# Dense matmuls over all 128 rows beside windowed attention, with six PSUM banks for the attention and one mask per block

## The chip, the core and the metric

The kernel runs on one NeuronCore of a Trainium2 chip. The metric is the device time of one execution, in microseconds (us). Below, PE is the matrix engine, PEld its weight loads, DVE the vector engine, ACT the scalar engine, POOL the GpSimd engine, SP the engine whose queue issues most DMAs. PSUM has eight banks of 128 x 512 fp32, into which PE writes.

## What is computed

```
x = A_x                                        # 1 x 2048 x 512
g = sigmoid((x * gate_w).sum(-1))
a = x @ dft_hid_re.T ;  b = x @ dft_hid_im.T
A = dft_seq_re @ a - dft_seq_im @ b            # real part of a 2-D DFT
q, k, v = split(x @ wqkv)                      # 32 heads of 16
p = softmax(q k^T / 4, over keys 0..255 back)  # causal window of 256
B = (p v) @ wo
out = g * A + (1 - g) * B
```

## The kernel before

**Precision.** Every dense product is made from high and low parts: three matmuls per contraction chunk (`TERMS`), so a 128 x 512 result over 512 contractions takes twelve "terms" into one accumulator. `hi_of` makes the high part on ACT, `lo_of` the low part on DVE or POOL.

**Dense work** is a generator, `dense()`. It makes the q, k, v projections, then the hidden-dimension DFT (`b_group`, `a_group`), then 32 blocks of the sequence DFT (`c_block`, with `piece_load` and `piece_split` to bring and split the DFT matrix). One `next()` on the generator is one term. At the end `wo_run` multiplies by `wo`.

**Attention** runs in 128 block steps (8 groups of 4 heads times 16 blocks of 128 queries); `n` counts them. In step `n`, `s_head` makes the scores S of four heads for block `n` (a matmul of 48 rows in the upper or the lower 64 rows of PE), and a DVE instruction adds the window mask and takes the row extreme. Every fourth step `m_rows` turns the extremes of four blocks into rows: DVE, then a write to a small DRAM tile `m_scr`, then a read of it into two rows of `ring`. `LAG` = 9 steps later `t_head` makes the transposed scores T of the same block, whose matmul has 50 rows and adds the extreme by those two rows. ACT takes the exponential into `pt`, POOL zeroes what lies outside the window (`t_mask`), and every fourth step `pv` multiplies by v (96 small matmuls of 64 x 32, tile `o`).

**Beside attention** the dense terms are put between the S and T matmuls by `fill`: 16 terms in a step while `n < LAG`, 11.2 while the projections last, 5 during the sequence DFT. While the flag `rows[0]` is set, a term is two matmuls of 64 rows (upper and lower half of PE) into two PSUM banks; `collect` copies one bank by ACT and then DVE adds the other. Before and after attention a term is one matmul of 128 rows into one bank.

**PSUM.** Pool `ps_a` has four banks for S, T and the two sums of `pv`; pool `ps_d` has four for the dense accumulators.

**Order.** Instructions stand on each engine in the order in which the Python code issues them, and every engine works its list in order. `defer(t, f)` puts a function `t` ticks later; a dense term is one tick, a group of S and T adds 0.7, `pv` adds 9. `ld` issues a DMA on SP, and an SP entry whose condition isn't met holds up those behind it.

Of the kernel before, what the change touches and what calls it, by code (L numbers as in the profile page):

```python
# [15 lines left out]
P = 128  # L16
# [5 lines left out]
NH = 4  # L22
# [28 lines left out]
def fnet_window_mix(ctx: ExitStack, tc: tile.TileContext, xT, x, wqk, wv, wr, wi, cr, ci, wo, gw, out):  # L51
# [170 lines left out]
    rows = [False]  # L222
    turn = 0

    def acc():
        nonlocal turn
        if rows[0]:
            return [ps_d.tile([P, 512], F32, name=f"d{h}", tag=f"d{h}", bufs=2) for h in range(2)]
        turn ^= 1
        return [ps_d.tile([P, 512], F32, name="d0", tag=f"d{turn ^ 1}", bufs=2)]  # L230

    def mm(pss, w, x, start, stop):
        if len(pss) == 1:
            nc.tensor.matmul(pss[0], w, x, start=start, stop=stop)  # L234
        else:
            for h in range(2):
                r = slice(64 * h, 64 * h + 64)
                nc.tensor.matmul(pss[h], w[r], x[r], start=start, stop=stop)  # L238
        tick()

    def collect(pss, then, scale=1.0, tag="es"):
        t = pt_tile([P, 512]) if len(pss) == 1 else ev.tile([P, 512], F32, name=tag, bufs=3 if tag == "es" else 5)
        nc.scalar.activation(t, pss[0], AF.Copy, scale=scale)  # L243

        def add():
            nc.vector.scalar_tensor_tensor(t, pss[1], scale, t, op0=OP.mult, op1=OP.add)
            defer(3, then, t)
        if len(pss) == 1:
            defer(3, then, t)
        else:  # L250
            defer(3, add)

    def evict_split(pss, hi, lo, scale, done, pool=True):
# [7 lines left out]
        collect(pss, first, scale)  # L261

    def qk_evict(g, ss, i, pss):
# [6 lines left out]
        evict_split(pss, hl[:, 1 - i], hl[:, i], (-SCALE, 1.0)[i], done, i == 1)  # L270

# [11 lines left out]
    def qk_proj(g, ss, w):  # L283
        for i in range(2):
            pss = acc()
            n = 0
            for dk in range(DK):
                c = dk * 256 + i * 128
                for a, b in TERMS:
                    mm(pss, w[a][:, c:c + 128], XT[dk, ss][:, b], n == 0, n == 11)  # L290
                    n += 1
                    if n < 12:
                        yield
            qk_evict(g, ss, i, pss)
            yield
# [9 lines left out]

    def row_proj(sb, w, pss):
        n = 0
        ss, c = divmod(sb, 4)
        for dk in range(DK):
            wh = [w[dk // 2][h][:, (dk % 2) * 512:(dk % 2) * 512 + 512] for h in range(2)]  # L310
            for a, b in TERMS:
                mm(pss, XT[dk, ss][:, a, c * 128:(c + 1) * 128], wh[b], n == 0, n == 11)
                n += 1
                if n < 12:
                    yield

    def v_proj(sb, w):
        pss = acc()
        yield from row_proj(sb, w, pss)

        def done(t):
            (nc.sync if rows[0] else nc.scalar).dma_start(v_scr[sb // 4][sb % 4], t)
            have.add(("v", sb))
        collect(pss, done)
        yield
# [10 lines left out]
    def quarter_block(i, q, j, w, then):  # L336
        pss = acc()
        yield from row_proj(q + 4 * j, w, pss)
# [5 lines left out]
        collect(pss, kept, (1.0, -1.0)[i], "es" if j % 2 else "ev")  # L344
        yield
# [103 lines left out]
    def m_rows(u):  # L449
# [49 lines left out]

    def t_mask(n, p):  # L500
        w = min(WIN, S - n % NB * P)
        pt = PT[n]
        a = pt[:, 2 * p:2 * p + 2, 0:P]
        nc.gpsimd.affine_select(a, a, pattern=[[0, 2], [1, P]], compare_op=OP.is_ge, fill=0.0,  # L504
                                base=0, channel_multiplier=-1)
        if w == WIN:
            a = pt[:, 2 * p:2 * p + 2, 2 * P:3 * P]
            nc.gpsimd.affine_select(a, a, pattern=[[0, 2], [-1, P]], compare_op=OP.is_gt, fill=0.0,  # L508
                                    base=0, channel_multiplier=1)

    def pv(u, last=False):
# [17 lines left out]
        nc.scalar.copy(os, ot[0])  # L529
        defer(3, lambda: nc.vector.tensor_add(os, ot[1], os))  # L530
        hf = g // 4
# [26 lines left out]
        defer(7, o_out)  # L558

# [33 lines left out]
    def piece_split(n, at_=1, step=2):  # L593
# [8 lines left out]
        for k, j in enumerate((2, 1, 3)):  # L602
            d, src, sign = left(i, tb, raws, j)
            defer(at_ + step * k, minus if sign > 0 else plus, d, d, src, j != 3)
        defer(at_ + step * 3, lo_of, w[:, 0], main, hi, True)
        for k, d in enumerate((raws[0][:, HALVES[1]], raws[1])):
# [22 lines left out]
    def c_block(n, done, begin):  # L629
        i, tb = order[n]  # L630
        pss = acc()
        hl = PIECE.pop((i, tb))
        begin(tb)
        for m in range(12):
            q, t = divmod(m, 3)
            x, y = TERMS[t]
            mm(pss, hl[x][:, q * P:q * P + P], U[i, tb % 4, q][:, y], m == 0, m == 11)
            if m < 11:
                yield
        if FIN:  # L640
            wo_run()
        done(tb, pss)
        piece_split(n + 2, 2, 2)
# [5 lines left out]
    def dense():  # L649
# [82 lines left out]

        def store_r(tb, pss):
            t = ev.tile([P, 512], F32, name="ev")
            nc.scalar.activation(t, pss[0], AF.Copy, scale=g1[:, tb:tb + 1])

            def add():
                nc.vector.scalar_tensor_tensor(t, pss[1], g1[:, tb:tb + 1], t, op0=OP.mult, op1=OP.add)
            if len(pss) == 2:
                defer(3, add)  # L740
            defer(7, ld, r_scr[0][tb], t)

# [5 lines left out]

        def add_r(tb, pss):
            r = R.pop(tb)  # L750
            for ps in pss:
                nc.vector.scalar_tensor_tensor(r, ps, g1[:, tb:tb + 1], r, op0=OP.mult, op1=OP.add)
            if FIN and tb in (11, 15):
# [90 lines left out]
    def wo_run():  # L844
# [11 lines left out]
        for q in range(0, 512, w):  # L856
# [3 lines left out]
            for g in range(NG):  # L860
                for a, b in TERMS:
                    mm([ps[:, :w]], OHL[sb][g][:, a, c * P:(c + 1) * P], WO[g][b][:, k], n == 0, n == 11)
                    n += 1
# [47 lines left out]
    for n in range(N + LAG + 1):  # L911
        k = n - LAG
        ring_ahead(n + 1)
        if k in (-2, 0):
            v_ahead(k // 2 + 1)
        for p in range(NH):
            if 0 <= k < N > n:
                s_head(n, p)
                t_head(k, p ^ 1)
            elif p % 2 == 0:  # L920
                for j in range(p, p + 2):
                    if n < N:
                        s_head(n, j)
                    elif k < N:
                        t_head(k, j)
# [6 lines left out]
            if p == 2 and k % 4 == 0:  # L932
                if k >= 4:
# [14 lines left out]
    with tc.If(small < 1):  # L948
        OTHER.clear()
        QT = {}  # L950
        for i in range(2):
# [6 lines left out]
            for tb in range(16):  # L958
                raws = raw_tiles(i, tb)
                dh, dl = (pt_tile([P, 3, 512], F32R) for _ in range(2))  # L960
                for j in (1, 2, 3):
# [3 lines left out]
                    lo_of(dl[:, j - 1], d, dh[:, j - 1])  # L965
                pss = acc()
                for n in range(36):
                    q, j = n % 4, n // 4 % 3
                    x, y = TERMS[n // 12]
                    mm(pss, (dh, dl)[x][:, j, q * P:q * P + P], QT[i, j, q][:, y], n == 0, n == 35)  # L970
# [3 lines left out]
                nc.vector.scalar_tensor_tensor(r, pss[0], g1[:, tb:tb + 1], r, op0=OP.mult, op1=OP.add)  # L974
                ld(o, r)
# [45 lines left out]
```

## Time and profile before

| | |
|---|---|
| median of 3 runs | 777.09 us (772.69 to 777.9) |
| the profiled execution: its own time | 772.52 us |
| the profiled execution: span from first to last instruction | 770.8 us |
| PE busy | 650.1 us, 84% of the span |
| DVE / ACT / POOL busy | 544.1 / 437.8 / 470.4 us |
| mean granted PE clock | 0.906 |
| DMA | 174.36 MB, mean 226 GB/s |

The time outside the span is 1.7 us. Busy times overlap, and the busy time of PE includes the modelled tail of each matmul, so that it overstates what PE does. The span has four stages, by what runs beside attention: start-up to 34.6 us; attention's first nine steps, S alone, to 71.4; attention beside projections and the hidden DFT to 353.8; attention beside the sequence DFT to 677; then the rest without attention.

### The profile page before, as it was taken

What the parts mean: (1) busy time and instruction counts of PE and PEld (TensorE: products, weight loads), DVE (VectorE), ACT (ScalarE), POOL (GpSimd) and SP (SyncE); (2) the same over time, 40 slices, a digit from 0 to 9 for tenths busy, and PEclk for the clock granted to TensorE, in tenths of its full rate; (3) what the DMA queues carried; (4) which work ended last, traced back from release to release, by engine and by line L of the source; (5) the groups of instructions that cost most, each with busy time, mean ns of one, the idle gap of its engine ahead of it and who ended that gap; (6) DMA issues with size and microseconds to landing.
All of it is one profiled execution on the core that took longest, in us unless ns stands there. A gap on an engine that the chain in (4) does not pass through costs nothing.

```text
span 770.8 us, 18841 instructions
## 1 busy us (share of the span) xinstructions
PE 650.1 (84%) x6558; PEld 499.8 (65%) x6558; DVE 544.1 (71%) x1471; ACT 437.8 (57%) x928; POOL 470.4 (61%) x718
## 2 busy tenths in 40 slices
PE   9999999899999999978677978878887687835976
PEld 6788887777788777766455655655555456624754
DVE  5388878898897889768567757676678863516554
ACT  6334775455576545666577657656756567514230
POOL 5002565667667878787768859796875869822000
PEclk9999999999999999989789879978978868975979
DMA  7857775777666877798868678885877648697675
GB/s 281 264 171 221 221 233 174 214 215 219 212 206 194 236 211 216 251 277 251 254 182 248 220 203 248 263 247 148 269 205 242 209 162 301 233 297 259 189 249 155
DMA packets 99994, 174.36 MB, mean 226 GB/s; under 512 B 34420, under 2 KB 35316, under 8 KB 99764
## 3 DMA queue, kind: packets, MB, share of 16 engines
q1 hardware_dynamic: 98452, 170.98, 72.2%
q10 hardware_dynamic: 1440, 2.10, 0.8%
q8 instruction: 54, 0.88, 0.5%
q14 instruction: 48, 0.39, 0.2%
HBM read 114.03 MB, written 63.46 MB: 230 GB/s over the span
## 4 chain that ended last, share of the span: by engine, by line
DMA 18%; PE 17%; POOL 8%; DVE 8%; issue 6%; SPq 4%; ACT 3%; DVEq 0%; POOLq 0%; ACTq 0%
DMA ring<-m_scr 5%; PE d L238 5%; SPq L97 4%; PE t L234 4%; DVE sm L445 3%; PE o L523 3%; DMA raw<-cr 3%; DMA ring<-qk_scr 3%; PE t L497 2%; DMA pt<-o_scr 2%; PE s L442 2%; POOL pt L504 1%; POOL hl L106 1%; DMA hl<-cr 1%; DMA ev<-wo 1%
## 5 line engine op out<-in xcount | busy, mean ns | idle before, releaser
L445 DVE CUSTOM_DVE_ANT_0 sm<-s,mask 128x384 f32<-128x384 f32 (+2 forms) x512 | 269.8, 527 | 87.0 <-PE s L442 41.9
L498 ACT ACTIVATE pt<-t 128x384 f32<-128x384 f32 (+2 forms) x512 | 234.2, 475 | 131.8 <-PE t L497 93.7
L497 PE MATMUL t<-ring,ring 50*128 50x384 f32 (+2 forms) x512 | 199.9, 400 | 56.6 <-DMA ring<-m_scr 32.0
L442 PE MATMUL s<-ring,ring 48*128 48x384 f32 (+2 forms) x512 | 185.0, 372 | 24.2 <-DVE nm L445 22.5
L504 POOL TENSOR_SCALAR_AFFINE_SELECT pt<-pt 128x256 f32<-128x256 f32 x256 | 116.0, 454 | 124.2 <-ACT pt L498 117.0
L238 PE MATMUL d<-big,hl 64*128 64x512 f32 x896 | 171.8, 421 | 0.0
L497 PEld LDWEIGHTS t<-ring,ring 50*128 50x128 f32 x512 | 101.9, 202 | 89.0 <-issue 26.5
L442 PEld LDWEIGHTS s<-ring,ring 48*128 48x128 f32 x512 | 99.4, 198 | 78.7 <-DVE nm L445 66.3
L238 PE MATMUL d<-hl,big 64*128 64x512 f32 x984 | 147.9, 395 | 0.0
L238 PE MATMUL d<-big,es 64*128 64x512 f32 x448 | 122.7, 473 | 0.0
L238 PEld LDWEIGHTS d<-big,hl 64*128 64x128 f32 x896 | 110.0, 198 | 5.2 <-issue 0.6
L238 PEld LDWEIGHTS d<-hl,big 64*128 64x128 f32 x984 | 105.2, 186 | 6.9 <-issue 0.8
L508 POOL TENSOR_SCALAR_AFFINE_SELECT pt<-pt 128x256 f32<-128x256 f32 x224 | 95.3, 425 | 0.0
L523 PE MATMUL o<-pt,vpad 64*32 64x320 f32 (+5 forms) x2816 | 83.3, 373 | 5.9 <-DVE nm L445 3.7
L523 PEld LDWEIGHTS o<-pt,vpad 64*32 64x32 f32 x2816 | 66.6, 113 | 28.1 <-DVE nm L445 10.3
L238 PEld LDWEIGHTS d<-big,es 64*128 64x128 f32 x448 | 66.3, 224 | 2.5 <-issue 0.6
L106 POOL TENSOR_TENSOR hl<-es,hl 128x512 fp32r<-128x512 f32 x14 | 19.0, 1359 | 65.2 <-ACT hl L103 61.6
L529 ACT COPY os<-o 128x512 f32<-128x512 f32 x32 | 18.8, 587 | 64.2 <-PE o L523 64.2
L530 DVE TENSOR_TENSOR os<-o,os 128x512 f32<-128x512 f32 x32 | 22.1, 690 | 42.8 <-ACT os L529 38.8
L106 POOL TENSOR_TENSOR hl<-raw,es 128x512 fp32r<-128x512 f32 x32 | 44.0, 1375 | 0.0
L243 ACT ACTIVATE es<-d 128x512 f32<-128x512 f32 x53 | 31.7, 598 | 19.8 <-PE d L238 19.0
L106 POOL TENSOR_TENSOR big<-big 128x512 fp32r<-128x512 f32 x32 | 41.6, 1304 | 0.2 <-ACT big L103 0.2
(100 smaller groups left out, 902.5 us busy)
## 6 DMA issues: line engine op xcount, KB each, us to landing
qk_scr<-hl SPq DMA_DIRECT2D x32, 512.0 KB
ring<-qk_scr SPq DMA_DIRECT2D x128, 128.0 KB
ring<-qk_scr SPq DMA_DIRECT2D x128, 64.0 KB
u_scr<-os SPq DMA_DIRECT2D x32, 256.0 KB
raw<-cr SPq DMA_DIRECT2D x16, 512.0 KB
big<-cr SPq DMA_DIRECT2D x16, 512.0 KB
raw<-ci SPq DMA_DIRECT2D x16, 512.0 KB
big<-ci SPq DMA_DIRECT2D x16, 512.0 KB
```

The source lines that it names most:

```text
L97: nc.sync.dma_start(dst, src)
L106: (nc.gpsimd if pool else nc.vector).tensor_sub(lo, raw, f(hi))
L234: nc.tensor.matmul(pss[0], w, x, start=start, stop=stop)
L238: nc.tensor.matmul(pss[h], w[r], x[r], start=start, stop=stop)
L243: nc.scalar.activation(t, pss[0], AF.Copy, scale=scale)
L442: nc.tensor.matmul(ps[:, :w], ring[0][r, p, jb * P:(jb + 1) * P], ring[1][r, p, k0:k0 + w], start=True, stop=True)
L445: nc.vector.tensor_tensor_reduce(out=sm[:, :w], in0=ps[:, :w], in1=mask[:, WIN - w:], scale=1.0, scalar=3e38, op0=OP.add, op1=OP.min, accu ...
L497: nc.tensor.matmul(ps[:, :w], ring[1][r, p, q0:q0 + P], ring[0][r, p, q0:q0 + w], start=True, stop=True)
L498: nc.scalar.activation(pt[:, j, :w], ps[:, :w], AF.Exp, scale=-1.0)
L504: nc.gpsimd.affine_select(a, a, pattern=[[0, 2], [1, P]], compare_op=OP.is_ge, fill=0.0, base=0, channel_multiplier=-1)
L508: nc.gpsimd.affine_select(a, a, pattern=[[0, 2], [-1, P]], compare_op=OP.is_gt, fill=0.0, base=0, channel_multiplier=1)
L523: nc.tensor.matmul(ot[h][32 * j:32 * j + 32, a - sb * 512:e - sb * 512], v2[r, j], pt[r, j, a - kb * P:e - kb * P], start=kb == kbs[0], st ...
```

## The change

1. A dense term is one matmul of 128 rows into one bank all the time; the DVE addition of the second half is gone (`mm`, `collect`, `store_r`, `add_r`). The pool `ps_d` has two banks.
2. `ps_a` has six banks.
3. A step has two groups and not four: each issues S, T, S, T for two heads and then the dense terms of half a step (`fill` adds `2 * rate` once per group).
4. `t_mask` masks four heads at once: two POOL instructions of 4 x 128 per row and step where four of 2 x 128 were.
5. The reads of `m_scr` into `ring` are issued on ACT and not on SP.
6. Some delays move: the addition of the two `pv` sums from 3 to 5 ticks, its store from 7 to 9; in `piece_split` the low part is taken before the sums and differences.

```diff
-    ps_a = ctx.enter_context(tc.tile_pool(name="ps_a", bufs=4, space=PSUM))
+    ps_a = ctx.enter_context(tc.tile_pool(name="ps_a", bufs=6, space=PSUM))
...
     def acc():
-        nonlocal turn
-        if rows[0]:
-            return [ps_d.tile([P, 512], F32, name=f"d{h}", tag=f"d{h}", bufs=2) for h in range(2)]
-        turn ^= 1
-        return [ps_d.tile([P, 512], F32, name="d0", tag=f"d{turn ^ 1}", bufs=2)]
-
-    def mm(pss, w, x, start, stop):
-        if len(pss) == 1:
-            nc.tensor.matmul(pss[0], w, x, start=start, stop=stop)
-        else:
-            for h in range(2):
-                r = slice(64 * h, 64 * h + 64)
-                nc.tensor.matmul(pss[h], w[r], x[r], start=start, stop=stop)
+        return ps_d.tile([P, 512], F32, name="d")
+
+    def mm(ps, w, x, start, stop):
+        nc.tensor.matmul(ps, w, x, start=start, stop=stop)
         tick()
...
-        nc.scalar.activation(t, pss[0], AF.Copy, scale=scale)
-
-        def add():
-            nc.vector.scalar_tensor_tensor(t, pss[1], scale, t, op0=OP.mult, op1=OP.add)
-            defer(3, then, t)
...
+        nc.scalar.activation(t, ps, AF.Copy, scale=scale)
+        defer(3, then, t)
...
                 for h in range(2):
-                    ld(f(ring[0][64 * h + 48:64 * h + 50, :, b % NB * P:b % NB * P + (e - b) * P]),
-                       ms[:, h, :, o:o + e - b].rearrange("l p b i q -> l p (b i q)"))
+                    nc.scalar.dma_start(f(ring[0][64 * h + 48:64 * h + 50, :, b % NB * P:b % NB * P + (e - b) * P]),
+                                        ms[:, h, :, o:o + e - b].rearrange("l p b i q -> l p (b i q)"))
...
-    def t_mask(n, p):
+    def t_mask(n):
...
-        a = pt[:, 2 * p:2 * p + 2, 0:P]
-        nc.gpsimd.affine_select(a, a, pattern=[[0, 2], [1, P]], compare_op=OP.is_ge, fill=0.0,
+        a = pt[:, :, 0:P]
+        nc.gpsimd.affine_select(a, a, pattern=[[0, 4], [1, P]], compare_op=OP.is_ge, fill=0.0,
                                 base=0, channel_multiplier=-1)
...
         def add_r(tb, ps):
             r = R.pop(tb)
-            for ps in pss:
-                nc.vector.scalar_tensor_tensor(r, ps, g1[:, tb:tb + 1], r, op0=OP.mult, op1=OP.add)
+            nc.vector.scalar_tensor_tensor(r, ps, g1[:, tb:tb + 1], r, op0=OP.mult, op1=OP.add)
...
-        quota += rate / 2
+        quota += 2 * rate
...
-        for p in range(NH):
-            if 0 <= k < N > n:
-                s_head(n, p)
-                t_head(k, p ^ 1)
...
-            if p % 2 and 0 <= k < N:
-                defer(2, t_mask, k, p // 2)
-            tick(0.7)
-            fill(n)
...
+        for p in (0, 2):
+            for j in (p, p + 1):
+                if n < N:
+                    s_head(n, j)
+                if 0 <= k < N:
+                    t_head(k, j ^ 1)
+            tick(1.4)
+            if p and 0 <= k < N:
+                defer(4, t_mask, k)
```

On PE in the stage of the projections, before: `s` and `t` are S and T, and two neighbouring numbers of `d` are the two banks of one dense accumulator, so each term is a row with the lower number and one with the higher.

```order
L442 MATMUL s<-ring_281,ring_280 128x384
L497 MATMUL t<-ring_280,ring_281 128x384
L238 MATMUL d_5172<-hl,big 128x512
L238 MATMUL d_5173<-hl,big 128x512
L238 MATMUL d_5172<-hl,big 128x512
L238 MATMUL d_5173<-hl,big 128x512
L238 MATMUL d_5241<-hl,big 128x512
L238 MATMUL d_5242<-hl,big 128x512
L442 MATMUL s<-ring_281,ring_280 128x384
```

The same engine and stage with the change; a row with x6 is six terms, each of 128 rows.

```order
L227 MATMUL d<-big,hl 128x512 x6
L424 MATMUL s<-ring_281,ring_280 128x384
L479 MATMUL t<-ring_280,ring_281 128x384
L424 MATMUL s<-ring_281,ring_280 128x384
L479 MATMUL t<-ring_280,ring_281 128x384
L227 MATMUL d<-big,hl 128x512 x5
```

Where PE had matmuls in one half of its rows throughout, it now goes from 128-row terms to four half-row matmuls and back, twice in a step.

On SP in the stage of the sequence DFT, before: from the write of one `m_scr` tile to its read.

```order
L97 DMA m_scr_179<-mt 4x32x32
L97 DMA u_scr_1_203<-os 128x512
L97 DMA vr<-v_scr_110 128x4x64
L97 DMA r_scr_3_213<-ev 128x512
L97 DMA raw<-cr 128x1024
L97 DMA big<-cr 128x1024
L97 DMA hl<-ci 128x512
L97 DMA ring_280<-m_scr_179 2x2x512 x2
L97 DMA ring_280<-qk_scr_3_3_93 32x2x512
```

The read of the same tile with the change stands on ACT, among the exponentials (`pt<-t`) and the casts:

```order
L103 CAST es<-raw 128x512
L480 ACTIVATE pt<-t 128x384 x2
L103 CAST big<-big 128x512
L480 ACTIVATE pt<-t 128x256 x2
L450 DMA ring_280<-m_scr_179 2x2x512 x2
L480 ACTIVATE pt<-t 128x256 x2
L103 CAST big<-big 128x512
```

The read has left SP's list, where it stood behind three loads of the DFT matrix (512, 512 and 256 KB by the profile's list of DMAs), and now stands between exponentials on ACT.

More of the change, by code (lines that the diff above doesn't have):

```diff
@@ L222, in fnet_window_mix, with collect, evict_split @@
     rows = [False]
-    turn = 0
     def acc():
-        nonlocal turn
-        if rows[0]:
-            return [ps_d.tile([P, 512], F32, name=f"d{h}", tag=f"d{h}", bufs=2) for h in range(2)]
-        turn ^= 1
-        return [ps_d.tile([P, 512], F32, name="d0", tag=f"d{turn ^ 1}", bufs=2)]
-    def mm(pss, w, x, start, stop):
-        if len(pss) == 1:
-            nc.tensor.matmul(pss[0], w, x, start=start, stop=stop)
-        else:
-            for h in range(2):
-                r = slice(64 * h, 64 * h + 64)
-                nc.tensor.matmul(pss[h], w[r], x[r], start=start, stop=stop)
-        tick()
-    def collect(pss, then, scale=1.0, tag="es"):
-        t = pt_tile([P, 512]) if len(pss) == 1 else ev.tile([P, 512], F32, name=tag, bufs=3 if tag == "es" else 5)
-        nc.scalar.activation(t, pss[0], AF.Copy, scale=scale)
-        def add():
-            nc.vector.scalar_tensor_tensor(t, pss[1], scale, t, op0=OP.mult, op1=OP.add)
-            defer(3, then, t)
[L248 to L253, printed above, removed]
+        return ps_d.tile([P, 512], F32, name="d")
+    def mm(ps, w, x, start, stop):
+        nc.tensor.matmul(ps, w, x, start=start, stop=stop)
+        tick()
+    def collect(ps, then, scale=1.0, tag="es"):
+        t = ev.tile([P, 512], F32, name=tag, bufs=3 if tag == "es" else 5) if rows[0] else pt_tile([P, 512])
+        nc.scalar.activation(t, ps, AF.Copy, scale=scale)
+        defer(3, then, t)
+    def evict_split(ps, hi, lo, scale, done, pool=True):
         def first(t):
@@ L260, in second, with qk_evict @@
             defer(6, done)
-        collect(pss, first, scale)
-    def qk_evict(g, ss, i, pss):
+        collect(ps, first, scale)
+    def qk_evict(g, ss, i, ps):
         hl = ev.tile([P, 2, 512], F32R, name="hl", bufs=3)
@@ L284, in qk_proj @@
         for i in range(2):
-            pss = acc()
+            ps = acc()
             n = 0
@@ L293, in qk_proj @@
                         yield
-            qk_evict(g, ss, i, pss)
+            qk_evict(g, ss, i, ps)
             yield
@@ L317, in v_proj @@
     def v_proj(sb, w):
-        pss = acc()
-        yield from row_proj(sb, w, pss)
+        ps = acc()
+        yield from row_proj(sb, w, ps)
         def done(t):
@@ L323, in done @@
             have.add(("v", sb))
-        collect(pss, done)
+        collect(ps, done)
         yield
@@ L336, in quarter_block @@
     def quarter_block(i, q, j, w, then):
-        pss = acc()
-        yield from row_proj(q + 4 * j, w, pss)
+        ps = acc()
+        yield from row_proj(q + 4 * j, w, ps)
         def kept(t):
@@ L343, in kept @@
             then(t)
[L344 removed]
+        collect(ps, kept, (1.0, -1.0)[i], "es" if j % 2 else "ev")
         yield
@@ L603, in piece_split @@
             d, src, sign = left(i, tb, raws, j)
-            defer(at_ + step * k, minus if sign > 0 else plus, d, d, src, j != 3)
-        defer(at_ + step * 3, lo_of, w[:, 0], main, hi, True)
+            defer(at_ + step * (k + 2), minus if sign > 0 else plus, d, d, src, j != 3)
+        defer(at_ + step, lo_of, w[:, 0], main, hi, True)
         for k, d in enumerate((raws[0][:, HALVES[1]], raws[1])):
@@ L630, in c_block @@
         i, tb = order[n]
-        pss = acc()
+        ps = acc()
         hl = PIECE.pop((i, tb))
@@ L641, in c_block @@
             wo_run()
-        done(tb, pss)
+        done(tb, ps)
         piece_split(n + 2, 2, 2)
@@ L731, in begin_0, with store_r @@
             pass
-        def store_r(tb, pss):
+        def store_r(tb, ps):
             t = ev.tile([P, 512], F32, name="ev")
[L735 to L741, printed above, removed]
+            nc.scalar.activation(t, ps, AF.Copy, scale=g1[:, tb:tb + 1])
+            defer(5, ld, r_scr[0][tb], t)
         R = {}
@@ L915, in fnet_window_mix @@
             v_ahead(k // 2 + 1)
-        for p in range(NH):
-            if 0 <= k < N > n:
-                s_head(n, p)
-                t_head(k, p ^ 1)
[L920 to L925, printed above, removed]
-            if p % 2 and 0 <= k < N:
-                defer(2, t_mask, k, p // 2)
-            tick(0.7)
-            fill(n)
+        for p in (0, 2):
[7 more added lines that the diff above has]
+                defer(4, t_mask, k)
             if p == 0 and k % 4 == 0 and k // 4 - 1 in ML:
                 defer(3, m_rows, k // 4 - 1)
-            if p == 2 and k % 4 == 0:
+            if p and k % 4 == 0:
                 if k >= 4:
@@ L973, in fnet_window_mix @@
                 ld(r, o)
-                nc.vector.scalar_tensor_tensor(r, pss[0], g1[:, tb:tb + 1], r, op0=OP.mult, op1=OP.add)
+                nc.vector.scalar_tensor_tensor(r, ps, g1[:, tb:tb + 1], r, op0=OP.mult, op1=OP.add)
                 ld(o, r)
```

26 lines of the change are left out of this document (13 added, 13 removed).

## The prediction

> **What bounds the kernel now.** I read the busy times by stage first, and in the same windows the S matmuls, the dense terms and the sums of v (columns: window, its length, busy us and count, granted clock, DMA share, GB/s).
>
> ```profile
> core 0: us, PE busy (x) PEld busy (x) DVE busy (x) ACT busy (x) POOL busy (x), PEclk, DMA share, GB/s
> 34.60:71.38 36.78, 36.78 (x315) 30.64 (x316) 29.78 (x97) 12.69 (x23) 2.93 (x3) 1.00 0.66 215
> 71.38:353.80 282.42, 261.74 (x3201) 219.99 (x3198) 236.31 (x692) 176.00 (x374) 199.18 (x321) 0.99 0.72 217
> 353.80:677.00 323.20, 255.82 (x2692) 177.99 (x2688) 218.75 (x598) 207.19 (x474) 248.75 (x377) 0.85 0.76 230
> ...
> 71.38:353.80 282.42, 84.60 (x248) 0.99 0.72 217
> 353.80:677.00 323.20, 93.16 (x228) 0.85 0.76 230
> ...
> 71.38:353.80 282.42, 218.40 (x1392) 0.99 0.72 217
> 353.80:677.00 323.20, 169.38 (x672) 0.85 0.76 230
> ...
> 71.38:353.80 282.42, 34.66 (x1312) 0.99 0.72 217
> 353.80:677.00 323.20, 48.62 (x1504) 0.85 0.76 230
> ```
>
> The first window (S alone) is all PE. In the second (projections) PE and DVE are both above 80% busy, at full clock. In the third (sequence DFT) nobody is above 79%, and the clock is 0.85. Four S make a step: 62 steps in the second window, 57 in the third, plus nine of T alone. What PE really works is found from starts, not from busy time. The timeline of PE has the three forms side by side:
>
> ```profile
> 34.66 0.33 PE L442 MATMUL s<-ring,ring 48*128 48x128 f32 x2
> 34.92 2.10 PE L234 MATMUL d<-hl,big 128*128 128x512 f32 x8
> 36.96 0.33 PE L442 MATMUL s<-ring,ring 48*128 48x128 f32 x2
> ...
> 41.34 0.28 PE L442 MATMUL s<-ring,ring 48*128 48x256 f32 x2
> 41.46 2.03 PE L238 MATMUL d<-big,hl 64*128 64x512 f32 x16
> ...
> 47.34 0.34 PE L442 MATMUL s<-ring,ring 48*128 48x384 f32 x2
> 47.52 1.99 PE L238 MATMUL d<-hl,big 64*128 64x512 f32 x16
> 49.34 0.34 PE L442 MATMUL s<-ring,ring 48*128 48x384 f32 x2
> ...
> 121.72 2.42 PE L523 MATMUL o<-pt,vpad 64*32 64x64 f32 x96
> 124.07 0.50 PE L238 MATMUL d<-hl,big 64*128 64x512 f32 x2
> ```
>
> From 47.34 on, everything is in half rows: two S of 384 columns start 0.18 us ahead of the dense terms, and eight terms (x16) take 1.82 us, **0.228 each**. At 41.34 two S of 256 columns take 0.12, so two of 128 take 0.06. The first group is just what the change makes everywhere: two S of 128 columns, then eight terms of 128 rows. It takes 36.96 - 34.66 = 2.30 us; in half rows it would be 0.06 + 1.82 = 1.88. **Leaving the 128-row form and coming back costs 0.42 us a group**, some 0.21 a switch. The terms themselves cost the same: two half-row matmuls of a pair run at once.
>
> So PE works, in the second window, 696 terms x 0.228 + 248 pairs of S and T x 0.18 + 14 pv (1312 / 96) x 2.5 (121.72 to 124.07, and the switch behind it) = 159 + 45 + 35 = 239 of 282 us, and idles 43. In the third, 336 x 0.228 + 264 x 0.18 + 16 x 2.5 = 164 at full clock, 193 at 0.85, of 323. What PE waits for, in the second window and then in the third, and the chain of the third:
>
> ```profile
> PEld s L442 <- DVE nm L445: 21.5, 38, 1.4
> PEld t L497 <- DVE nm L445: 7.6, 9, 2.2
> ...
> PE t L497 <- DMA ring<-m_scr: 27.6, 11, 7.0
> PEld s L442 <- DVE nm L445: 44.8, 94, 4.1
> POOL pt L504 <- ACT pt L498: 58.3, 41, 4.6
> ...
> by line: DMA ring<-m_scr 12.8%; issue 10.8%; SPq L97 8.9%; PE d L238 7.6%; PE o L523 7.2%; DVE sm L445 5.4%; PE t L497 4.8%; DMA ring<-qk_scr 3.5%; PE s L442 3.1%; POOL pt L504 2.9%; ACT pt L498 2.3%; POOL pt L508 2.2%; DVE ev L752 2.2%; PO
> ```
>
> In the projections PE waits mostly for a bank that DVE has not read. In the sequence DFT the dearest link is the read of `m_scr`, in front of T; PE's own work is 22.7% of the chain, 73 us.
>
> **The switches (added).** A step has two groups, each out of the 128-row form and back. A step with `pv` goes term, S and T, `pv`, term: three switches there, where before it had two.
> - First window: 9 steps x 2 x 0.42 = 7.6. PE is busy without a gap, so all of it counts: **+7**. The ends are 0 and +8.
> - Second: 62 x 4 - 14 = 234 switches x 0.21 = 49 us. PE would work 239 + 49 = 288 us in a window of 282, so it can't be hidden whole. PE becomes the only bound, and the 43 us of idling shrink: the waits for banks (29 us in the two rows above) are what the six banks and a lighter DVE take away. I leave 12 us of idling: 300, **+18**. The ends are +6 (no idling) and +49 (all idling stays).
> - Third: 132 groups x 2 - 16 = 248 x 0.21 = 52, at clock 0.85 61 us. Of PE's 193 us here 73 are on the chain, 38%; the same share of the switches is **+23**. The ends are 0 (hidden in PE's 130 us of idling) and +61.
>
> The Trainium skill ("TensorEngine Tiling", Key Properties) says that a change of tiling mode drains the array, a change of tile within it does not; that speaks against this change. Its "TensorE: Matmul & The Clock Gate" puts a load of 128 columns at 107 ns (LDWEIGHTS) and the drain at some 175 ns (Single matmul latency); from these one switch is an estimated 0.28 us, by which the second window's 49 us would be 66. Here the trace agrees that the array drains, but has 0.42 us for two, and that is used.
>
> **Taken from DVE.** The second halves' additions go:
>
> ```profile
> L246 DVE SCALAR_TENSOR_TENSOR es<-d,es 128x512 f32<-128x512 f32 x53 | 36.3, 685 | 3.3 <-ACT es L243 3.0 <-PE d L238 0.3
> L738 DVE SCALAR_TENSOR_TENSOR ev<-d,g,ev 128x512 f32<-128x512 f32 x16 | 11.9, 745 | 0.0
> L752 DVE SCALAR_TENSOR_TENSOR ev<-d,g,ev 128x512 f32<-128x512 f32 x28 | 20.8, 742 | 23.3 <-PE d L238 8.8 <-DMA ev<-r_scr 6.8 <-DMA lt<-l_scr 5.0
> ```
>
> In the projections that is 53 x 0.685 and 16 more of the same: 47 us of DVE's 236, which lies beside PE's 288 and so shortens nothing by itself; it is counted in the shrunk idling. In the third window all of L738 and twelve of L752's 28 go, 21 us of 219, and with the latter part of their 2.2% of the chain (7 us): **-4**; the ends are 0 and -7.
>
> **Six banks.** In the third window S waits 44.8 us for DVE, but only 5.4% of the chain (17 us) is DVE's reduction. More banks move the wait and don't make DVE faster: **-5**; the ends are 0 and -17.
>
> **The read of `m_scr` on ACT.** Two pieces of the chain of the third window, the slow case and the fast one, and what SP waited for:
>
> ```profile
> 394.26 5.55 DMA ring<-m_scr
> ...
> 473.27 1.59 DMA ring<-m_scr
> ...
> SPq L97 <- DMA m_scr<-mt: 18.6, 14, 3.2
> ...
> q1 hardware_dynamic: 98452, 170.98, 72.2%
> q10 hardware_dynamic: 1440, 2.10, 0.8%
> ...
> L322 ACTq DMA_DIRECT2D v_scr<-pt x6: 326/326/361, 15.7 to 34.7; - x6
> ```
>
> The same 8 KB take 5.55 us from issue to landing behind other loads and 1.59 alone. ACT's DMAs are in a queue of their own (q10), nearly empty. If the read lands in 1.6 us, eleven waits of 27.6 us in all shrink by up to 3-4 us each: **-22**, leaving the tail of the 7.0. The ends are 0 (it waits in the same 16 engines) and -41, its whole 12.8%. What is added: 80 issues of some 0.33 us in ACT's list, 26 us where ACT is 64% busy, beside PE; and ACT now stands still until the write has landed, with exponentials behind it, whose banks PE's T needs. The read is 12 ticks behind the write, in the third window more than a step (323 / 66 = 4.9 us), so I cost it at nothing; if ACT arrives as early as SP did, it is the 18.6 us of SP's row.
>
> The Trainium skill ("DMA: Bandwidth & Descriptors", Issuing engines are not separate DMA queues) says that all issuers' DMAs run on the same 16 engines and that another issuer saves issue time only. By that the -22 would be nearly 0, and the whole sum some 22 higher; the two rows of the chain show a spread to win, but no read from ACT beside heavy loads.
>
> **One mask for four heads.** These are the sizes that the trace has:
>
> ```profile
> L504 POOL TENSOR_SCALAR_AFFINE_SELECT pt<-pt 128x256 f32<-128x256 f32 x256 | 116.0, 454 | 124.2 <-ACT pt L498 117.0 <-DMA ring<-qk_scr 7.0
> L186 POOL TENSOR_SCALAR_AFFINE_SELECT mask<-mask 128x384 f32<-128x384 f32 x1 | 0.6, 646 | 0.1
> L188 POOL TENSOR_SCALAR_AFFINE_SELECT mask<-mask 128x384 f32<-128x384 f32 x1 | 0.8, 845 | 0.1
> ```
>
> From 0.454 us for 256 columns and 0.646 or 0.845 for 384, 512 columns are bounded by 0.65 (no further growth) and 1.24 (the steeper slope on). Against two of 0.454 that is -0.26 to +0.33 for each of 240 masks, -62 to +79 us of POOL. I take no change, the middle: the gentler slope gives 0.84. What POOL may gain is its standing before masks whose exponentials aren't there (58.3 us in the third window), since the one mask comes later. It is 77% busy there, and its masks are 5.1% of the chain, 16 us; 0.65 or 1.24 in place of 0.91 would make that -5 or +6, and the value is 0.
>
> **Moved delays and two accumulators instead of four** in the last stage: a block of twelve terms takes 2.7 us, an eviction 0.74. Nothing.
>
> **Sum**, against the profiled execution: 772.5 + 7 + 18 + 23 - 4 - 5 - 22 = 789.5. The runs' median, 777.09, is 4.6 above that execution, which is as fast as the fastest run; I add half of it: **792 us**.
>
> **Rivals.**
> - *The sequence DFT gains more than PE loses.* PE idles 130 of 323 us there, so the switches may hide whole, while the reads and banks give all they cost: -27.6 and -17 and -4, about -49, held by POOL's 249 busy us. With +7 and +6 ahead of it: 772.5 - 36 + 2 = 739. It decides from the point at which the third window falls by more than the first two grow (25 us): then the kernel is faster. For it: the clock is 0.85 because PE stands still there, and each removed wait also keeps the clock up. Against it: PE's matmuls stand in one list, and a switch delays the S that DVE waits for. Chance 0.20; its milder part, 745 to 767.
> - *A switch is cheaper behind wider matmuls.* The price comes from S of 128 columns; S and T are mostly 384 wide, and if the weights load while they run, only one switch in two costs: +4, +0 (263 us of PE work in 282), +11 - 31 in the third, 758. Against it: the switch from S to terms shows a load at its full price after the drain. Chance 0.06.
> - *ACT stands still.* The read waits on ACT as on SP, 18.6 us, and lands no sooner: no -22, so 792 + 41 = 833. Chance 0.10.
> - *The terms cancel*: the second window at its lower end (+6) and the third at -14: within 1%. Chance 0.14.
> - The forecast, slower by 8 to 50 us: 0.50.
>
> **How the numbers follow.** One per cent (7.8 us) is about what a measurement of this kernel can tell from no change. Faster by more: 0.20 + 0.06 = 0.26. Within: 0.14. Slower: 0.50 + 0.10 = 0.60. For 8 in 10 the range reaches from the milder part of the first rival to ACT's standing still: 750 to 833. The forecast's own range is 785 to 825.
>
> **What would show it.** The window of S alone should last 44 us and not 37; a group of S and T in the projections should stand 0.42 us of switches; PE should have hardly a gap there, and that window should last 288 to 310 us. T's waits for `m_scr` should be under 8 us. Wrong would be: a projection window no longer than 282 us (then a switch is cheaper than 0.21, or PE was worked out too high), a wait of ACT for `m_scr`, or a third window under 298.

## The result, and the profile after

The changed kernel takes **835.69 us** (median of 4 runs, 833.13 to 842.68) against 777.5 for the kernel before on the same chip: 1.078 times as long (95% interval 1.070 to 1.086). The forecast of 792 had the right sign, but it had 15 us of growth where 58 came, so three quarters of it are missing; the time lies above the range.

The busy times by stage, in the columns of the table shown of before (in order: S alone, projections, sequence DFT, the rest):

```profile
35.00:78.20 43.20, 43.20 (x183) 28.99 (x182) 24.56 (x87) 12.73 (x24) 2.92 (x3) 1.00 0.58 187
78.20:400.80 322.60, 303.14 (x2505) 195.39 (x2504) 209.98 (x632) 167.37 (x373) 180.21 (x203) 0.96 0.67 195
400.80:744.00 343.20, 309.22 (x2356) 174.87 (x2355) 199.21 (x571) 205.31 (x474) 231.59 (x254) 0.74 0.70 213
744.00:835.30 91.30, 61.45 (x230) 46.00 (x230) 44.39 (x63) 23.56 (x28) 9.05 (x7) 0.82 0.73 231
```

The three stages of attention grew by 6.4, 40.2 and 20.0 us, the rest fell by 2.5. In the projections and the sequence DFT PE is busier, and DVE, ACT and POOL are less busy. One plain step of the projections, from PE's timeline:

```profile
86.28 0.44 PE L424 MATMUL s<-ring,ring 48*128 48x384 f32 x1
86.28 0.44 PE L479 MATMUL t<-ring,ring 50*128 50x384 f32 x1
86.56 0.34 PE L424 MATMUL s<-ring,ring 48*128 48x384 f32 x1
86.56 0.34 PE L479 MATMUL t<-ring,ring 50*128 50x384 f32 x1
86.83 1.42 PE L227 MATMUL d<-big,hl 128*128 128x512 f32 x5
88.17 0.44 PE L424 MATMUL s<-ring,ring 48*128 48x384 f32 x1
...
90.31 0.44 PE L424 MATMUL s<-ring,ring 48*128 48x384 f32 x1
```

From 86.28 to 88.17 are 1.89 us for five terms (5 x 0.228 = 1.14) and two pairs of S and T (0.17 each, being 384 of a term's 512 columns): 0.41 are left, the price of one group's two switches, with S and T 384 columns wide. The whole step is 90.31 - 86.28 = 4.03. Half of the steps in that stage last no longer than 4.26; much of the stage's loss stands in longer ones. Here is the longest, first on PE, then on ACT, then on SP:

```profile
362.25 0.44 PE L479 MATMUL t<-ring,ring 50*128 50x384 f32 x1
371.22 0.69 PE L424 MATMUL s<-ring,ring 48*128 48x384 f32 x1 [8.53 <-ACT pt L480]
...
359.39 0.60 ACT L232 ACTIVATE es<-d 128x512 f32<-128x512 f32 x1
368.89 1.16 ACTq L450 DMA_DIRECT2D ring<-m_scr  x4
370.16 0.62 ACT L103 CAST hl<-es 128x512 fp32r<-128x512 f32 x1 [10.16 <-DMA vr<-v_scr]
...
355.64 6.79 SPq L97 DMA_DIRECT2D ring<-qk_scr  x8
364.71 0.58 SPq L97 DMA_DIRECT2D m_scr<-mt  x1
```

SP was stuck in loads of `ring` and issued the write of `m_scr` only at 364.71. ACT had reached the read of that tile at 359.99 and stood until the write had landed, at 368.89. Behind the read stand the exponentials, so no bank came free, and PE stood 8.5 us. (ACT's idle time is put down to another DMA there, since that one ended last.) Over all 33 reads ACT was idle 43 us just ahead of the read, nearly all of it in the projections (39 us), where it is 1 to 4 us at most of them; in the sequence DFT it was 1 us. The landing of the write, "DMA m_scr<-mt", is 7.1% of the chain of the projections, 23 us.

The waits and the chain in the sequence DFT:

```profile
PE t L479 <- DMA ring<-m_scr: 12.1, 5, 3.7
PEld s L424 <- DVE nm L427: 29.8, 47, 1.4
...
by line: PE d L227 23.6%; PE o L505 9.8%; PE s L424 9.5%; PE t L479 7.6%; issue 7.4%; DMA ring<-m_scr 6.4%; DVE sm L427 3.9%; ACT big L548 2.8%; DMA ring<-qk_scr 2.2%; SPq L97 2.2%; ACT pt L480 2.1%; POOL hl L106 1.7%; POOL raw L310 1.6%; P
...
445.55 4.29 DMA ring<-m_scr
506.07 3.79 DMA ring<-m_scr
```

PE's own work is half of the chain now (it was 22.7%). A read issued from ACT takes 3.8 to 5.0 us to land, about what one from SP took.

### The profile page after: what moved, and what is told of

Its sections match the earlier page's. It is cut to its first block, busy times and chain, and to the rows that moved or that the text cites. A ratio compares the mean times of both kernels' runs of the same rounds, so it can differ in the third digit from the quotient of the medians.

```text
span 835.3 us, 16193 instructions
## 1 busy us (share of the span) xinstructions
PE 750.3 (90%) x5394; PEld 470.2 (56%) x5394; DVE 491.9 (59%) x1374; ACT 427.1 (51%) x928; POOL 434.7 (52%) x478
## 4 chain that ended last, share of the span: by engine, by line
PE 55%; DMA 16%; DVE 8%; issue 8%; POOL 5%; ACT 4%; SPq 3%; ACTq 1%; DVEq 0%; POOLq 0%
PE d L227 33%; PE s L424 9%; PE o L505 6%; PE t L479 5%; DMA pt<-o_scr 4%; DMA m_scr<-mt 3%; DMA ring<-m_scr 3%; DVE sm L427 3%; SPq L97 3%; DMA ring<-qk_scr 2%; ACT pt L480 1%; PE t L227 1%; POOL hl L106 1%; ACT big L548 1%; DMA o_scr<-u_scr 1%
## 5 line engine op out<-in xcount | busy, mean ns | idle before, releaser
L480 ACT ACTIVATE pt<-t 128x384 f32<-128x384 f32 (+2 forms) x512 | 213.4, 473 | 156.1 <-PE t L479 114.3
L479 PE MATMUL t<-ring,ring 50*128 50x384 f32 (+2 forms) x512 | 184.8, 446 | 28.0 <-DMA ring<-m_scr 12.1
L227 PE MATMUL d<-big,hl 128*128 128x512 f32 x506 | 176.9, 451 | 0.9 <-POOL hl L106 0.5
L227 PE MATMUL d<-hl,big 128*128 128x512 f32 x576 | 158.9, 413 | 0.5 <-ACT pt L232 0.5
L486 POOL TENSOR_SCALAR_AFFINE_SELECT pt<-pt 128x512 f32<-128x512 f32 x128 | 90.8, 710 | 113.0 <-ACT pt L480 112.8
L227 PE MATMUL d<-big,es 128*128 128x512 f32 x256 | 123.5, 542 | 14.9 <-ACT es L103 14.9
L227 PEld LDWEIGHTS d<-hl,big 128*128 128x128 f32 x576 | 102.8, 190 | 36.7 <-issue 16.9
L227 PEld LDWEIGHTS d<-big,hl 128*128 128x128 f32 x506 | 99.7, 206 | 42.1 <-issue 21.8
L479 PEld LDWEIGHTS t<-ring,ring 50*128 50x128 f32 x512 | 90.0, 214 | 49.0 <-ACT pt L480 17.5
L227 PEld LDWEIGHTS d<-big,es 128*128 128x128 f32 x256 | 57.5, 243 | 43.4 <-issue 21.9
L490 POOL TENSOR_SCALAR_AFFINE_SELECT pt<-pt 128x512 f32<-128x512 f32 x112 | 74.9, 669 | 0.0
```

Of the source, the lines that this page charges most:

```text
L227: nc.tensor.matmul(ps, w, x, start=start, stop=stop)
L479: nc.tensor.matmul(ps[:, :w], ring[1][r, p, q0:q0 + P], ring[0][r, p, q0:q0 + w], start=True, stop=True)
L480: nc.scalar.activation(pt[:, j, :w], ps[:, :w], AF.Exp, scale=-1.0)
L486: nc.gpsimd.affine_select(a, a, pattern=[[0, 4], [1, P]], compare_op=OP.is_ge, fill=0.0, base=0, channel_multiplier=-1)
L490: nc.gpsimd.affine_select(a, a, pattern=[[0, 4], [-1, P]], compare_op=OP.is_gt, fill=0.0, base=0, channel_multiplier=1)
```

## The experiments

All are timed against the kernel before, on the same chip within a batch. Stages by starts in the profile: S alone from the first S to that of step 9, projections on to step 71, sequence DFT on to the last T.

| kernel | time, us | ratio to before (95%) | S alone | projections | sequence DFT |
|---|---|---|---|---|---|
| before | 777.5 | 1 | 36.7 | 282.4 | 310.1 |
| changed | 835.7 | 1.078 (1.070 to 1.086) | 43.1 | 322.6 | 330.4 |
| e1 changed, reads on SP | 787.7 | 1.014 (1.001 to 1.027) | 43.1 | 292.8 | 313.5 |
| e2 before, reads on ACT | 804.4 | 1.040 (1.024 to 1.055) | 38.9 | 313.3 | 304.2 |
| e3 e1 with half rows, 4 + 4 banks | 799.5 | 1.034 (1.024 to 1.044) | 37.3 | 319.8 | 303.0 |
| e4 e1 with four groups | 871.9 | 1.129 (1.118 to 1.140) | 43.1 | 340.5 | 346.7 |
| e5 changed, reads at 20 ticks | 831.5 | 1.067 (1.059 to 1.074) | 43.1 | 299.8 | 338.2 |
| e6 e1 with four banks | 828.9 | 1.065 (1.058 to 1.071) | 43.1 | 313.6 | 324.3 |
| e7 before, one mask | 770.7 | 0.990 (0.985 to 0.996) | 36.7 | 281.6 | 307.9 |
| e8 before, reads on ACT at 20 | 801.0 | 1.030 (1.024 to 1.036) | 36.7 | 300.2 | 327.7 |
| e9 changed, reads at 20, then 6 | 793.6 | 1.028 (1.021 to 1.035) | 43.1 | 298.4 | 311.2 |
| e10 e7 with the moved delays | 775.1 | 1.001 (0.997 to 1.005) | 36.7 | 280.1 | 314.5 |
| e11 e7, early read on SP | 760.1 | 0.982 (0.978 to 0.987) | 36.7 | 283.1 | 292.4 |
| e12 e1, early read on SP | 787.6 | 1.014 (1.005 to 1.022) | 43.1 | 295.1 | 305.2 |

The four runs of e1 lie from 778.8 to 790.6, and its profile is of the longest, so its stages are upper ends. In the batches the kernel before took 775.9 to 778.2 us.

**e1, the reads back on SP.**

```diff
-                    nc.scalar.dma_start(f(ring[0][...]), ms[...])
+                    ld(f(ring[0][...]), ms[...])
```

> The changed kernel with the reads of m_scr issued on SP again; all else as changed. In the changed kernel's trace ACT stands 43 us in front of those reads, nearly all of it in the window of the projections, which grew by 40 us where 18 were forecast. Theory A (standing ACT is the missing part): the projections' window falls from 323 to about 300 us and the time from 836 to 805 to 815. Theory B (the switches alone, and ACT's standing lies beside PE): within 1% of 836. Theory C (the read from ACT pays in the sequence DFT): the window behind the projections grows by 10 to 20 us, so that the time is 825 to 840.

This one edit is worth 48 of the change's 58 us. The projections, the sequence DFT (the window that corresponds to 400.80 to 744.00 above) and T's waits for `m_scr` in e1:

```profile
78.20:371.00 292.80, 288.13 (x2503) 187.52 (x2502) 208.35 (x632) 169.41 (x373) 180.24 (x203) 1.00 0.72 210
371.00:697.60 326.60, 298.74 (x2356) 169.42 (x2355) 196.56 (x571) 204.54 (x475) 232.83 (x254) 0.76 0.75 227
...
PE t L479: 10.3, 4
```

The projections last 292.8 us where PE's work had been put at 288, and T waits for `m_scr` no more than with the reads on ACT (10.3 in place of 12.1). So the read from ACT gained nothing, and it cost 30 us in the projections. Compared step by step, the long step above takes 4.03 us in e1 and not 14.73, and a dozen others are 0.9 to 3.5 us shorter. Theory A has it, and by more than was expected: the projections came to 293 us for about 300, the time to 788 for 805 to 815.

The sequence DFT is 17 us shorter in e1, and what made that is not shown. ACT had stood only 1 us there, and T's waits are alike. PE's busy time times the granted clock is nearly the same (309.22 x 0.74 = 229, 298.74 x 0.76 = 227), so 10 of the 17 us go with a lower clock; whether the reads on ACT lowered it is open.

**e2, the same edit in the kernel before.**

```diff
-                    ld(f(ring[0][...]), ms[...])
+                    nc.scalar.dma_start(f(ring[0][...]), ms[...])
```

> The kernel before with one edit: the reads of m_scr on ACT. Theory A (ACT stands until the write has landed): slower by 10 to 30 us, the loss in the projections, where 12 ticks are less than a step. Theory C (the read lands sooner from an empty queue): the window of the sequence DFT shrinks by 15 to 25 us, with T's waits for m_scr under 10 us instead of 27.6; the sum is then within 1% or faster.

Both effects show, and the loss wins: +31 us in the projections, -6 in the sequence DFT. ACT stood 46 us ahead of the reads. T's waits for `m_scr` fell from 32.0 us to 11.6 over the whole run. The edit alone makes the kernel before 4% slower.

**e5 and e8, the read later on ACT; e9, its place by stage.**

```diff
-            defer(12, read)
+            defer(20, read)                                  # e5; e8 on top of e2
+            defer(6 if "proj" in have else 20, read)         # e9
```

> The changed kernel with one number moved: the read of m_scr, still on ACT, stands 20 ticks behind the write and not 12. Moving the reads to SP took 48 us off. Theory A1 (ACT stands because it meets the read before the write has landed, and its exponentials behind it stop PE): at 20 ticks the write has landed, ACT's idle time in front of the reads falls from 43 to under 10 us, the projections' window from 323 to 290 to 300, the time to 785 to 800. Theory A2 (the cost is that of issuing 80 DMAs from ACT, 0.27 us each, or of what they wait for besides the write): 815 or more.

> The kernel before with the reads of m_scr on ACT, 20 ticks behind the write and not 12 (with 12 it took 804.4 us). Theory A1: without the standing it is back at 770 to 782. Theory C (the read from ACT lands sooner and frees SP): below that, 755 to 770, by the window of the sequence DFT. Theory A2 (issuing from ACT costs by itself): 790 or more.

> The changed kernel with the reads of m_scr on ACT, 20 ticks behind the write while the projections last and 6 in the sequence DFT (12 in the changed kernel, 835.7 us). With 20 everywhere the projections' window fell from 323 to 300 us, but in the sequence DFT T waited 40 us for reads that ACT reached 9 to 14 us after the write. Theory: the cost of the read on ACT is its place in ACT's list alone, too early in one stage and too late in the other; with both mended the projections take 295 to 302 us, T's waits for m_scr in the sequence DFT fall under 10 us, and the time is 785 to 800, that of the reads on SP. Rival (a read on ACT costs in the sequence DFT wherever it stands): 805 or more.

In e5 and e8 some T of the sequence DFT are issued ahead of the read of their extremes and use older ones, since the nine ticks of `pv` pass in one go; their times there are read with that. The projections are clear: ACT's idle time ahead of the reads fell from 43 to 12 us, and the stage from 322.6 to 299.8 in e5. By the time alone, 831.5 us, theory A1 missed and A2 would hold. But 20 ticks are too late for the other stage. Who waited for `m_scr`, in e5 and then in e9:

```profile
PE t L479: 39.9, 14
ACT pt L480: 8.5, 1
...
ACT pt L480: 15.5, 3
ACT es L232: 4.7, 2
ACT ev L232: 2.1, 1
PE t L479: 0.8, 2
```

e9, with both places mended and every T behind its read, takes 793.6 us, as expected. So nearly all that the read on ACT costs comes from where it stands in ACT's list, not from being issued there; well placed it is no better than on SP. The 6 us that e9 takes more than e1 lie within the two intervals. e8 missed its forecast too (801.0 for 770 to 782): its sequence DFT is 18 us longer than before, with late reads as in e5 (T waited 36.4 us for `m_scr`), but its projections stayed 18 us longer as well, with ACT idle for 15 us ahead of the reads over the whole run. Why they did not come back whole was not tried.

**e4, twice as many switches.** The loop of before (four groups of one S and one T) on e1.

```diff
-        for p in (0, 2):
-            for j in (p, p + 1): ...
-            tick(1.4)
+        for p in range(NH):
+            s_head(n, p); t_head(k, p ^ 1)
+            tick(0.7)
```

> The changed kernel with the reads on SP and 128-row terms, but with the order of before: four groups in a step, each of one S and one T. That doubles the switches. Theory of the switches (0.42 us a group): two groups more in 62 steps of the projections are 52 us, in 9 steps of S alone none (there the order of before has two groups), in 66 steps of the sequence DFT 55 us at full clock, of which a third to all shows; 70 to 110 us slower than the kernel with two groups and the reads on SP. Rival (the price is a fixed one of 128-row terms, not of the switch): within 15 us of it.

It is 84 us slower than e1: nothing in the stage of S alone, where the number of groups is the same, 48 us in the projections (52 expected), 33 in the sequence DFT. On PE's timeline a group of three terms lasts 1.27 to 1.28 us:

```profile
91.55 0.44 PE L424 MATMUL s<-ring,ring 48*128 48x384 f32 x1
91.55 0.44 PE L479 MATMUL t<-ring,ring 50*128 50x384 f32 x1
91.92 0.97 PE L227 MATMUL d<-big,hl 128*128 128x512 f32 x3
92.83 0.44 PE L424 MATMUL s<-ring,ring 48*128 48x384 f32 x1
```

3 x 0.228 + 0.17 = 0.85; 0.42 are left again. The price hangs on the switch, not on the 128-row term.

**e3, half rows with all else of e1.** Dense terms in half rows, so that `ps_a` and `ps_d` have four banks each.

```diff
-    ps_a = ctx.enter_context(tc.tile_pool(name="ps_a", bufs=6, space=PSUM))
+    ps_a = ctx.enter_context(tc.tile_pool(name="ps_a", bufs=4, space=PSUM))
...   acc, mm, collect, store_r and add_r as before
```

> The changed kernel with its two groups in a step, its one mask and its delays, but with dense terms in half rows again (so four banks for dense accumulators, four for S, T and sums of v) and the reads of m_scr on SP. Theory of the switches: without 128-row terms there is no switch but those of pv, and the time is that of before, 765 to 790, some 35 us or more under the kernel with the same reads and 128-row terms. Rival (the wider groups or the one mask cost the time): 800 or more.

The theory missed: 799.5, 12 us *over* e1. Without switches the projections are 27 us longer than with them. The mask and the delays are no reason (e10 below, 775.1). What PE waited for longest in the projections of e3 is DVE's reading of S, ahead of `pv`, whose two sums need banks:

```profile
PE o L524 <- DVE nm L446: 23.7, 14, 4.4
```

Either the wide groups alone or their having only four banks had to be the reason; e6 keeps the groups and takes the banks away from e1.

**e6, 128-row terms with four banks.**

```diff
-    ps_a = ctx.enter_context(tc.tile_pool(name="ps_a", bufs=6, space=PSUM))
+    ps_a = ctx.enter_context(tc.tile_pool(name="ps_a", bufs=4, space=PSUM))
```

> The changed kernel with the reads on SP (787.7 us) and with four banks for S, T and sums of v instead of six; two banks of PSUM stay unused. Theory D (a group of two S and two T needs its banks free at once, and sums of v take two more): the projections' window grows by 20 to 35 us, as it did with half rows and four banks (320 us), and the time is 805 to 825. Rival (that version lost by half rows beside wide groups, not by banks): 780 to 795.

Two banks that stand idle cost 41 us (the forecast had 17 to 37), 21 of them in the projections. What S waits for there, in e6 and then in e1:

```profile
PEld s L424 <- DVE nm L427: 23.6, 61, 1.1
...
PEld s L424 <- DVE nm L427: 6.0, 13, 1.8
```

A group of S, T, S, T takes all four banks, and `pv` needs two more; with one S and one T in a group four had been enough. Wide groups halve the switches, but only with six banks, and with two accumulators for the dense work six banks only come free with 128-row terms. In this layout the three parts of the change hang together; half rows with a single accumulator were not tried.

**e7, one mask in the kernel before; e10, with the moved delays; e11, with an early read.**

```diff
-    def t_mask(n, p):
+    def t_mask(n):                                           # e7: 4 x 128 a row, once a step
...
-        defer(3, lambda: nc.vector.tensor_add(os, ot[1], os))
+        defer(5, lambda: nc.vector.tensor_add(os, ot[1], os)) # e10, with the other delays
...
-            defer(12, read)
+            defer(7 if "proj" in have else 12, read)         # e11, on SP
```

> The kernel before with one edit: one mask for four heads (two POOL instructions of 512 columns a step instead of four of 256), issued after the last group of the step. In the changed kernel's trace the two take 0.71 and 0.67 us where two pairs took 0.45 and 0.43 each: some 45 us of POOL's 470 go. Theory E (POOL paces the sequence DFT): 762 to 772, all of it in that window. Rival (POOL only follows ACT): within 1% of before, 770 to 782.

> The kernel before with the one mask for four heads (770.7 us by itself) and the moved delays of the changed kernel: sum of the pv halves at 5 ticks, its store at 9, the low part of a DFT piece ahead of its sums and differences. Half rows, four groups, reads on SP. Version with half rows, wide groups, the one mask and these delays had the shortest sequence DFT of all (264.5 us from its first to its last S, against 271.3 before). If the mask and the delays are the reason: that window 262 to 268 and the time 758 to 768. If the wide groups are: 766 to 775, as with the mask alone.

> The kernel before with the one mask, and the read of m_scr on SP 7 ticks behind the write in the sequence DFT and not 12, so that it stands ahead of some loads of the DFT matrix. If the 27.6 us of T's waits for m_scr are the read's late issue (4 to 7 us behind the write there): T waits under 15 us, the time 755 to 766. If SP's standing for the write holds the loads behind it up as much: 766 to 775.

The mask alone gives 1.0%. Its 770.7 us lie in the ranges of both theories, so e7 does not tell them apart. POOL's rows of e7:

```profile
L504 POOL TENSOR_SCALAR_AFFINE_SELECT pt<-pt 128x512 f32<-128x512 f32 x128 | 89.2, 697 | 132.3 <-ACT pt L498 122.4 <-DMA ring<-qk_scr 5.6 <-DVE nm L445 4.0
L508 POOL TENSOR_SCALAR_AFFINE_SELECT pt<-pt 128x512 f32<-128x512 f32 x112 | 76.7, 685 | 0.0
```

166 us where four smaller ones took 211. The delays (e10) add nothing and by the intervals take most of it back. The early read (e11) is what pays: T's waits for `m_scr` fall from 31.0 in e7 to 16.7 (under 15 was forecast), the sequence DFT by 16 us, and at **760.1 us** it beats both kernels by more than the intervals. Against e7 the ratios differ by 0.8%, and their intervals just overlap.

**e12, the early read with 128-row terms.** The edit of e11 on e1.

> The changed kernel with the reads of m_scr on SP (787.7 us with 12 ticks) and 7 ticks behind the write in the sequence DFT. With half rows the early read took T's waits for m_scr down and gave 760.1 us. With 128-row terms T waits only 10 us for m_scr, so less can be won: 775 to 786, that is 15 us or more over the half rows, which is then what 128-row terms, six banks and wide groups together cost against the best of the other side. Rival (the switches are covered once the reads are early): 765 or less.

No gain: 787.6 us, 2 above the forecast, though T's waits for `m_scr` fall to 2.8 us. The chains of the sequence DFT, in e12 and then in e11:

```profile
by line: PE d L227 24.1%; issue 12.0%; PE s L424 11.6%; PE t L479 7.6%; PE o L505 7.1%; DVE sm L427 3.6%; ACT pt L480 3.3%; ACT big L548 3.2%; DMA ring<-qk_scr 3.1%; SPq L97 2.5%; POOL raw L310 2.4%; POOL big L313 2.3%; DMA hl<-ci 2.1%; POO
...
by line: DVE sm L445 10.1%; issue 9.7%; PE d L238 9.5%; PE o L523 6.4%; DMA hl<-ci 6.4%; DMA ring<-m_scr 6.3%; SPq L97 5.9%; PE t L497 5.6%; PE s L442 4.8%; DMA m_scr<-mt 2.7%; ACT pt L498 2.5%; DVE ev L752 2.5%; DMA big<-cr 2.5%; ACT big L
```

With 128-row terms PE's matmuls are half of this chain (50.4%; in the projections of e12 they are 92%), with half rows a quarter (26.3%). T had waited only 10 us for `m_scr` in e1, against 31 in e7, so less could be won, and more of the time is PE's own work. Whether that is the whole reason was not tried. The 27.5 us between e12 and e11 (24 by their ratios to the kernel before) are what 128-row terms with their six banks, wide groups and delays cost against half rows, with the mask and the reads alike.

## Why the prediction was wrong

- **The switch: right.** 0.42 us a group was read from two groups of the first stage; 0.41 stands in the changed kernel's own steps and 0.42 in e4. S alone grew by 6.4 (7 forecast). The Trainium skill ("TensorEngine Tiling", Key Properties) names the drain, and the trace agrees with it.
- **Projections without the read: right in kind.** PE's work was put at 288 us and the stage at 300; e1 has 292.8. Idling shrank from 43 us to 5 and not to 12.
- **The failed step: "so I cost it at nothing".** The wait that the change puts into ACT's list was seen, with the exponentials behind it, and then covered by a count of ticks in the sequence DFT. In the projections a step has 14 ticks (11.2 terms and 2.8 for its groups; 23 with `pv`), so 12 ticks are less than a step, and SP's list, which holds the write, can be late by itself. That cost 30 us there. A wait of ACT for `m_scr` was one of the prediction's own signs of being wrong, and it showed. The 18.6 us of SP's row, which the prediction weighed for the third window, are of the whole run; by stage (S alone, projections, sequence DFT, in the kernel before) two thirds of them stand ahead of that window:

```profile
SPq L97 <- DMA m_scr<-mt: 3.8, 2, 2.2
...
SPq L97 <- DMA m_scr<-mt: 8.6, 10, 1.4
...
SPq L97 <- DMA m_scr<-mt: 6.1, 2, 3.2
```

The rival "ACT stands still" named this with a chance of 0.10. That its 833 us come so close to 835.7 is luck: it put 19 us of standing on a sum of 814, where the runs have 48 on 787.7, and the two errors cancel.

- **The -22 of the same edit: wrong.** The 1.59 us were taken for what an empty queue gives. Reads from ACT land in 3.8 to 5.0 us. The Trainium skill ("DMA: Bandwidth & Descriptors", Issuing engines are not separate DMA queues) says that all issuers' DMAs run on the same 16 engines, and the trace agrees with it. T's waits did fall, to 12 us, but in e1, without the edit, to 10; longer steps leave a read more time, which would explain it and was not tried by itself. In the kernel before (e2) the edit did shorten the sequence DFT, by 6 us, a quarter of the 22. Together the edit was put at -22 and measured +48.
- **The sequence DFT without the read: mis-sized.** +23 for switches, -4 and -5 for DVE's additions and banks made +14; e1 has +3. T's waits for `m_scr` were shorter there too, and the granted clock was lower; how much each weighs is not shown.
- **Six banks, "-5": mis-sized.** They were taken for a help to S's waits; e6 shows them worth 41 us beside wide groups, which run well only with them.
- **One mask, 0: nearly right in time** (e7: -1.0%); POOL's saving of 45 us lay inside the bounds.

Without the read on ACT the same sum would have been 814 against 787.7. By e1's profile it was 7 us too high in the projections and 11 in the sequence DFT, and the last stage, for which it had no change, is 2.6 us shorter.

## What to carry to other kernels

A wait moved to another engine's list is to be priced in every stage, by what stands behind it there and by how late its condition is at its worst, not at its mean. Parts of PE used in halves and in full don't mix freely: each change of form cost 0.2 us here, so count them per loop before merging two half-row matmuls into one. When one engine takes over most of the chain, gains elsewhere can vanish: the early read gave 1.4% beside half rows (770.7 to 760.1; 0.8% by the ratios) and nothing beside 128-row terms.

## What the runs showed of the hardware

- In the sequence DFT the granted clock of PE fell from 0.85 to 0.74 while its modelled busy time rose from 255.8 of 323.2 us to 309.2 of 343.2; e1 has 0.76 with 298.7 of 326.6. With 128-row terms less standing of PE thus went with a lower clock, against what the prediction's first rival argued; in e11, with half rows, it went with a higher one (0.87 with 239.2 of 292.6). What sets the clock was not tried.
- A mask of 512 columns takes 0.67 to 0.71 us on POOL against 0.43 to 0.45 for 256: the second half costs about 0.25.
- A DMA of 8 KB issued from ACT's own queue lands hardly sooner than from SP's busy one: 3.8 to 5.0 us in the changed kernel and 4.0 to 4.9 in e2, against 4.3 to 5.8 before (eight of the nine reads on the chain; the ninth is the one of 1.59).
